# Two layers of block-cached attention and gated MLP on one core: square-block turning on VectorE, a second place for MLP sums, one copy for the last values

## The chip, the cores and the metric

One core of one Trainium2 chip runs the whole program. The metric is the device time of one execution in microseconds, the median of several runs.

## What is computed

A decode step for a batch of 4 rows of 640 numbers, float32, through attention, MLP, attention, MLP, with the same weights in both layers. Each stage norms its input and adds its result to it:

```python
def _A_ref(x, k_cache, v_cache, wq, wo):        # 32 heads of 128, the last W = 1024 cached positions
    q = (x @ wq) -> [B, 32, 1, 128]
    scores = einsum(q, k_cache[:, :, Sk - W:]) * 128 ** -0.5
    o = einsum(softmax(scores), v_cache[:, :, Sk - W:])
    return o.reshape(B, 1, 32 * 128) @ wo
def _B_ref(x, W_gate, W_up, W_down):            # 1728 hidden columns
    gate, up = x @ W_gate, x @ W_up
    return ((gate * (gate > 0)) * up) @ W_down
x = A_x
x = x + _A_ref(_layernorm(x), ...); x = x + _B_ref(_layernorm(x), ...)
x = x + _A_ref(_layernorm(x), ...); x = x + _B_ref(_layernorm(x), ...)
```

## The kernel before

All weights and caches are laid out on the host as rows of 128 partitions: `heads` (queries, keys, values and output weights of the heads in the order of use), `kept` (the five last heads, in two groups K0 and K1) and `mlp`. One list, `plan`, holds 89 pieces of these rows in the order in which SP issues them, each with its place in one large on-chip tile, `store` (128 x 50,624 float32, so one column is 512 B over all partitions). `load()` (L211) issues the next piece as soon as the program order has freed its whole place; the framework's semaphores then hold SP until the last matmul that reads that place is through. A piece counts as landed as a whole.

Layer 0 streams `heads` in pieces of 16,000 columns through three places, then loads all of `kept` and uses it last. The kept heads stay for layer 1, which begins with them (`order`). So the first MLP has little room: seven places of together 7,040 columns, four of them inside the kept rows. Three of these (`AHEAD` 768 columns, `BACK` 1,728, `AWAY` 1,280) hold kept data that ScalarE first copies elsewhere, into `probs`, the PSUM tiles `ps`, `yy`, `po` (columns 128 on), `pp` (the upper halves of its two banks) and the two `banks`, and later back. The first MLP's 25,920 columns go through these places in 28 pieces of 640 to 1,344 columns. The pieces behind them are the first of layer 1's `heads`: five into the places that the MLP leaves (1,280, 1,280, 704, 768, 1,728 columns), the next into places that layer 1's queries free (1,152 and 1,280 columns at the query weights of K0 and K1), and then into those that its scores free (1,024, 2,048, 3,392, 4,096, ...).

Matmuls of all these go through one helper, `product` (L242), which splits a matmul where its columns lie in two pieces.

The work around the change, in program order on each engine:

- `normalized()` (L335 to L357): VectorE sums the rows (L342), TensorE averages, VectorE subtracts (L346, the result `xc` in `gates`), ScalarE squares and sums (L348), TensorE turns `xc` (L352 and L354, into `pp`), and VectorE copies the turned rows to `xT` (L356). The rows lie as four groups of 160 columns at partitions 0, 32, 64 and 96, four batch rows in each.
- `deviation(ss)` (L359): four small matmuls on the sum of squares (L334), a root on ScalarE (L362), a reciprocal on VectorE (L363). In attention it stands before the first `query`; in the MLP behind `gate(3)`.
- `forward()`: `gate(j)` for j = 3, 0, 1, 2 makes a block of gate and up columns in `pp[:, j % 2]`; `gated(j)` applies relu on ScalarE (L552) and the product on VectorE (L553); `hidden(j)` turns the result (TensorE L560, copy on VectorE L561); `down(j)` adds into `y`.
- `fill` (L325) and `busy` (L318) are matmuls without use, into `po`, in the stretches in which `waits[0]` is set.
- `values(..., last)`: the last weighted values are copied from `po` to `gates` by VectorE (L450) and ScalarE (L451), half each; then four transpositions (L470) and `project`.

Of the kernel before, what the change touches and what calls it, by code (L numbers as in the profile page):

```python
# [1 line left out]

# [5 lines left out]
F32 = mybir.dt.float32  # L8
# [54 lines left out]


AHEAD = KEPT * D, KEPT * D + 768
BACK = FRONT - 2 * KV - 1728, FRONT - 2 * KV
AWAY = BACK[0] - 1280, BACK[0]
HOME = 12864
FIRST, MOST = 32640, 16320
LAP = 3 * MOST + 1024  # L70


def size_of(what, i):
    return len(HEADS[i]) * D if what == "q" else D if what == "o" else KV


def spread(parts):
# [11 lines left out]

ROWS = {row: spread(parts) for row, parts in PARTS.items()}  # L90

WHERE = {part: (row, at) for row, (places, _, _) in ROWS.items() for part, at in places.items()}


@with_exitstack
def decode_kernel(ctx: ExitStack, tc: tile.TileContext, x, source, sel, out):
# [28 lines left out]

    def stretch(layer, lo, end, to):

        size = -(-(end - lo) // -(-(end - lo) // MOST) // 64) * 64
        while lo < end:
            hi = min(end, lo + size)  # L130
            if to + hi - lo > LAP:
                to = 0
            to = put(layer, "heads", to, lo, hi)
            lo = hi
        return to
# [23 lines left out]

    f, z, a, q, k = FRONT, STORE - D, AHEAD[0], AWAY[0], BACK[0]  # L160
    assert STORE - FRONT == 2 * 1280 + 64 + D
    gu = [(z, D), (f, 1280), (f + 1280, 1344), (a, 768), (k, 960), (k + 960, 768), (q, 1280)]
    gu_end = [(f, 1280), (f + 1280, 1280), (f + 2560, D)]
    wd = [(a, D), (k, 960), (k + 960, D), (q, 1280), *gu_end, (a, D), (k, D), (k + D, D)]
    lo = 0
# [4 lines left out]


    lo = HELD
    for to, n in (f, 1280), (f + 1280, 1280), (f + 2560, D + 64), (a, 768), (k, 1728):
        put(1, "heads", to, lo, lo + n)
        lo += n
    to = AHEAD[1]
    for n in 1152, 1280, 1024, 2048, 3392:
        to = put(1, "heads", to, lo, lo + n)
        lo += n
    assert to == HOME  # L180
# [94 lines left out]
    nc.scalar.dma_start(out=sel_sb, in_=sel)  # L275


    xT = const.tile([P, KC * B + 28], F32, name="xT")


    qT = const.tile([P, SIDE - 1 + SIDE * SIDE * B], F32, name="qT")
# [4 lines left out]

    ps = ps_s.tile([P, 2, 512], F32, name="ps")
    pp = ps_p.tile([P, 2, 512], F32, name="pp")
    po = ps_o.tile([P, 512], F32, name="po")
    nc.vector.memset(ps, 0.0)  # L290
    nc.vector.memset(po, 0.0)
# [45 lines left out]
    def normalized():  # L337

        ysb, xc, sq = probs[:, :QUARTER], gates[:, :QUARTER], gates[:, QUARTER:2 * QUARTER]
        waits[0] = True  # L340
        su = small.tile([P, 1], F32, name="su", bufs=1)
        nc.vector.tensor_reduce(su, y, axis=AX.X, op=ALU.add)  # L342
        nc.scalar.copy(ysb, y)
        busy(2)
        mu = mean(su)
        nc.vector.tensor_tensor(xc, ysb, mu.to_broadcast([P, QUARTER]), op=ALU.subtract)  # L346
        ss = small.tile([P, 1], F32, name="ss", bufs=1)
        nc.scalar.activation(sq, xc, AF.Square, accum_out=ss)  # L348
        fill(1)

        pt = pp[:, 0, :KC * 32].rearrange("p (c x) -> p c x", c=KC)
        nc.tensor.transpose(pt[:, :4], xc[:, :P], ident)  # L352
        for g in range(4):
            nc.tensor.matmul(pt[32 * g:32 * g + 32, 4, :B], xc[:, P:], ident[:, 32 * g:32 * g + B],  # L354
                             start=True, stop=True, tile_position=(0, 32 * g))
        nc.vector.tensor_copy(xT[:, :KC * B].rearrange("p (c b) -> p c b", b=B), pt[:, :, :B])  # L356
        return ss  # L357

    def deviation(ss):  # L359
# [17 lines left out]
    def query(layer, g, spread=False):  # L377


        n = len(HEADS[g]) * P  # L380
        qp[g] = bank(n)
        for c in range(KC - 1):
            product(qp[g][32 * c:32 * c + 32], xT[:, B * c:B * c + 32], *part(layer, "q", g, c * n, n),
                    start=True, stop=c > 0 and not spread, tile_position=(0, 32 * c))
        part_done(layer, "q", g, 0, (KC - 1) * n)
        c = KC - 1
        m = n // 4 if spread else n
        for a in range(n // m):
            product(qp[g][32 * a:32 * a + 32, a * m:a * m + m], xT[:, B * c:B * c + 32],
                    *part(layer, "q", g, c * n + a * m, m), start=False, stop=True, tile_position=(0, 32 * a))  # L390
        part_done(layer, "q", g, c * n, n)

# [13 lines left out]
    def scores(layer, g):  # L406
        n = len(HEADS[g])
        to = sc[g] = pp if layer and g == order[1][0] else ps
        for i, h in enumerate(HEADS[g]):
            for j in range(2):  # L410
                for b in range(B):
                    lo = (j * B + b) * 512
                    at = SIDE - 1 + SIDE * (B * i + b) - i
                    product(to[32 * b:32 * b + SIDE, j, :], qT[:, at:at + SIDE], *part(layer, "k", h, lo, 512),
                            start=i == 0, stop=i == n - 1, tile_position=(0, 32 * b))
                    part_done(layer, "k", h, lo, 512)
                    if to is pp and k0 + i * KV + lo < HOME + BACK[1] - BACK[0] <= k0 + i * KV + lo + 512:
                        nc.scalar.copy(store[:, HOME:HOME + 1024], ps.rearrange("p j n -> p (j n)"))
                        nc.scalar.copy(store[:, HOME + 1024:HOME + 1408], po[:, P:])
                        nc.scalar.copy(store[:, HOME + 1408:HOME + 1728], yy[:, QUARTER:3 * QUARTER])  # L420
        nm[g] = small.tile([P, 1], F32, name="nm")
        nc.vector.tensor_reduce(nm[g], to.rearrange("p j n -> p (j n)"), axis=AX.X, op=ALU.max, negate=True)  # L422

# [8 lines left out]
    def values(layer, g, last=False):  # L432
# [14 lines left out]
        if last:  # L447
            waits[0] = layer == 0
            fill(1, pp[:, 0])
            nc.vector.tensor_copy(gates[:, 2 * P:], po[:, 2 * P:])  # L450
            nc.scalar.copy(gates[:, :2 * P], po[:, :2 * P])  # L451
            if layer == 0:
                nc.scalar.copy(po[:, P:], store[:, BACK[0] + 1024:BACK[0] + 1408])
                nc.scalar.copy(pp[:, :, 256:], away[:, :512].rearrange("p (j n) -> p j n", j=2))
                free(*BACK)
        else:
            nc.scalar.copy(gates, po)  # L457

    def totals(g):
        so = bank(P)  # L460
# [23 lines left out]
    def attention(layer):  # L484
# [38 lines left out]
        values_turned(gs[-1])  # L523
        if layer == 0:
            for i in range(2):
                nc.scalar.copy(banks[i][:, P:], away[:, 512 + 384 * i:896 + 384 * i])
            free(*AWAY)
            project(layer, gs[-2])
        fill(1)
# [2 lines left out]
    def forward(layer):  # L532
# [3 lines left out]
        def gate(j):  # L536
            n, groups = (P, 4) if j < 3 else (64, 3)
            at = GU0 + j * GU if j < 3 else 0
            gus[j] = pp[:, j % 2, :2 * P]
            for c in range(KC):  # L540
                for g in range(groups):
                    lo = at + (c * groups + g) * 2 * n
                    product(gus[j][32 * g:32 * g + 32], xT[:, B * c:B * c + 32], layer, "mlp", lo, 2 * n,
                            start=c == 0, stop=c == KC - 1, tile_position=(0, 32 * g))
                    done(layer, "mlp", lo, 2 * n)

        def gated(j):
            n, p = (P, P) if j < 3 else (64, 96)
            gu = gus.pop(j)
            at = 256 * (j % 2)  # L550
            a, b = gates[:p, at:at + n], gates[:p, at + P:at + P + n]
            nc.scalar.activation(a, gu[:p, :n], AF.Relu, scale=rstd[:p])  # L552
            nc.vector.scalar_tensor_tensor(b, gu[:p, n:2 * n], rstd[:p], a, op0=ALU.mult, op1=ALU.mult)  # L553
            return b

        def hidden(j, h):
            hTs[j] = small.tile([P, 4, B], F32, name="hT", bufs=4)
            ph = bank(P).rearrange("p (f x) -> p f x", f=4)
            if j < 3:
                nc.tensor.transpose(ph, h, ident)  # L560
                nc.vector.tensor_copy(hTs[j], ph[:, :, :B])  # L561
                return

            for g, lo, f in (0, 0, 0), (1, 64, 0), (2, 0, 1), (2, 64, 1):
                nc.tensor.matmul(ph[lo:lo + 64, f, :B], h, ident[:96, 32 * g:32 * g + B],
                                 start=True, stop=True, tile_position=(0, lo))
            nc.vector.tensor_copy(hTs[j][:, :2], ph[:, :2, :B])

        def down(j, last=False):
            for f in range(4 if j < 3 else 1):  # L570
# [19 lines left out]
        waits[0] = layer == 0  # L590
        rstd = deviation(ss)
        go_on()
        fill(1)
        h = gated(3)
        for j, j1 in (3, 0), (0, 1), (1, 2):
            gate(j1)
            hidden(j, h)
            fill(1)
            h = gated(j1)
        down(3)  # L600
        down(0)
        hidden(2, h)
        if layer == 0:
            nc.scalar.copy(away[:, :512].rearrange("p (j n) -> p j n", j=2), pp[:, :, 256:])
            for i in range(2):
                nc.scalar.copy(away[:, 512 + 384 * i:896 + 384 * i], banks[i][:, P:])
            live[AWAY[0]:AWAY[1]] = [True] * 1280
        down(1)
        down(2, last=True)

# [63 lines left out]
```

## Time and profile before

| | |
|---|---|
| median of 3 runs | 732.33 us (731.74 to 732.71) |
| profiled execution | 734.14 us, of which span 732.4 us |
| busy: TensorE, VectorE, ScalarE | 445.4, 75.2, 54.2 us |
| moved by DMA | 311.19 MB, mean 425 GB/s |
| mean granted TensorE clock | 0.816 |

The span is the time from the first to the last instruction on the core; what lies around it is start and end of the program. All times in the rows are microseconds from the span's start. PEclk is the granted clock as a share of 2.4 GHz: 0.50 is 1.2 GHz, and values between are means over a stretch in which both occur.

### The profile page before, as it was taken

Reading aid. Unit: us, or ns where it says so; the run is one execution under the profiler, and the core shown is the slowest. Engines: PE = TensorE matmul, PEld = TensorE weight load, DVE = VectorE, ACT = ScalarE, POOL = GpSimd, SP = SyncE. Lnnn points to the kernel's source line nnn. Section 1 sums busy time; section 2 is a strip of 40 time slices with the busy share of each in tenths; the row PEclk is TensorE's granted clock in tenths of the full one; section 3 lists DMA queues with packets and bytes.
Section 4 is the critical chain, followed back from the end, with each engine's and each line's share of the span. In section 5 each row is a group of like instructions: output and inputs, shape, how many; then the busy total and the mean of one; then the engine's idle time right before and its main releaser. Section 6 shows DMA issues by size and latency. Waiting matters only on the chain.

```text
span 732.4 us, 8422 instructions
## 1 busy us (share of the span) xinstructions
PE 445.4 (61%) x3844; PEld 158.6 (22%) x3844; DVE 75.2 (10%) x279; ACT 54.2 (7%) x101; POOL 0.2 (0%) x4
## 2 busy tenths in 40 slices
PE   0845565655655554619879896365656555556576
PEld 0211112222112121103344241021121112112123
DVE  1111001010010101002101211001010010101011
ACT  0200000000000000001302210000000000000100
POOL 0000000000000000000000000000000000000000
PEclk9888887776777777759999999677787878778989
DMA  9999999999999999999999999999999999999996
GB/s 405 445 405 438 440 445 416 434 431 444 441 419 428 419 441 448 419 431 425 419 392 407 392 427 455 423 441 434 433 427 444 424 441 426 438 437 420 423 429 286
DMA packets 13291, 311.19 MB, mean 425 GB/s; under 512 B 1476, under 2 KB 1732, under 8 KB 6984
## 3 DMA queue, kind: packets, MB, share of 16 engines
q1 hardware_dynamic: 13104, 310.56, 98.9%
q8 instruction: 30, 0.49, 0.2%
q10 hardware_dynamic: 152, 0.09, 0.0%
q14 instruction: 5, 0.04, 0.0%
HBM read 310.57 MB, written 0.08 MB: 424 GB/s over the span
## 4 chain that ended last, share of the span: by engine, by line
DMA 73%; PE 22%; another core or an unknown queue 3%; DVE 1%; issue 1%; SPq 0%; ACT 0%; DVEq 0%; ACTq 0%
DMA store<-in_heads 57%; DMA store<-in_kept 9%; PE ps L242 9%; DMA store<-in_mlp 7%; PE po L242 6%; PE m L242 2%; PE pp L242 1%; PE y L242 1%; PE pp L430 1%; PE m L401 1%; PE m L470 0%; PE m L461 0%; DVE gates L394 0%; SPq L211 0%
## 5 line engine op out<-in xcount | busy, mean ns | idle before, releaser
L242 PE MATMUL po<-store,pT 128*16 128x512 f32 (+2 forms) x1044 | 155.4, 707 | 130.4 <-DMA store<-in_heads 125.0
L242 PE MATMUL ps<-store,qT 128*4 128x512 f32 (+3 forms) x1016 | 151.7, 682 | 109.9 <-DMA store<-in_heads 89.4
L242 PEld LDWEIGHTS po<-store,pT 128*16 128x16 f32 x1044 | 38.4, 110 | 234.3 <-DMA store<-in_heads 124.7
L242 PEld LDWEIGHTS ps<-store,qT 128*4 128x4 f32 x1016 | 36.3, 94 | 206.7 <-DMA store<-in_heads 99.9
L422 DVE TENSOR_REDUCE nm<-ps 128x1 f32<-128x1024 f32 x17 | 20.8, 1224 | 242.4 <-PE ps L242 242.4
L426 ACT ACTIVATE probs<-ps,nm 128x1024 f32<-128x1024 f32 x17 | 18.9, 1114 | 328.9 <-DVE nm L422 328.9
L242 PE MATMUL m<-store,xT 128*32 128x512 f32 (+5 forms) x152 | 30.3, 600 | 10.5 <-DMA store<-in_heads 10.5
L440 DVE COPY pT<-pp 128x16 f32<-128x16 f32 x128 | 17.1, 168 | 140.2 <-PE po L242 140.2
L457 ACT COPY gates<-po 128x512 f32<-128x512 f32 x16 | 9.4, 586 | 249.5 <-PE po L242 249.5
L242 PE MATMUL pp<-store,xT 128*32 128x256 f32 (+3 forms) x322 | 21.0, 371 | 7.4 <-DMA store<-in_mlp 3.5
L242 PE MATMUL y<-store,oT 128*4 128x160 f32 x512 | 23.3, 314 | 1.3 <-DVE oT L474 1.1
L430 PE MATMUL pp<-sel_sb,probs 128*128 128x128 f32 x144 | 20.4, 289 | 0.0
L430 PEld LDWEIGHTS pp<-sel_sb,probs 128*128 128x128 f32 x144 | 17.9, 150 | 0.0
L463 DVE RECIPROCAL r<-m 128x16 f32<-128x16 f32 x18 | 4.6, 258 | 129.1 <-PE m L461 129.1
L242 PEld LDWEIGHTS y<-store,oT 128*4 128x4 f32 x512 | 13.2, 90 | 9.3 <-issue 3.9
L394 DVE TENSOR_SCALAR gates<-m,rstd 128x512 f32<-128x512 f32 (+2 forms) x18 | 12.4, 690 | 26.6 <-PE m L242 26.6
L242 PEld LDWEIGHTS pp<-store,xT 128*32 128x32 f32 x322 | 11.3, 114 | 15.2 <-DMA store<-in_mlp 6.7
L401 PE MATMUL m<-sel_sb,gates 128*128 128x128 f32 x64 | 12.8, 325 | 0.0
L242 PE MATMUL y<-store,hT 128*4 128x160 f32 (+1 forms) x224 | 11.2, 299 | 2.4 <-DMA store<-in_mlp 2.2
L470 PE MATMUL m<-sel_sb,gates 128*128 128x128 f32 x72 | 12.0, 289 | 0.8 <-DVE gates L450 0.8
L401 PEld LDWEIGHTS m<-sel_sb,gates 128*128 128x128 f32 x64 | 7.9, 159 | 20.0 <-issue 20.0
L242 PEld LDWEIGHTS m<-store,xT 128*32 128x32 f32 x152 | 7.2, 124 | 22.3 <-DMA store<-in_heads 11.7
(80 smaller groups left out, 124.1 us busy)
## 6 DMA issues: line engine op xcount, KB each, us to landing
store<-in_heads SPq DMA_DIRECT2D x22, 8000.0 KB, 45.7
store<-in_heads SPq DMA_DIRECT2D x1, 7776.0 KB, 45.5
store<-in_heads SPq DMA_DIRECT2D x1, 7744.0 KB, 46.0
store<-in_heads SPq DMA_DIRECT2D x1, 7424.0 KB, 44.6
store<-in_heads SPq DMA_DIRECT2D x1, 7360.0 KB, 35.3
store<-in_heads SPq DMA_DIRECT2D x1, 7168.0 KB, 33.6
store<-in_mlp SPq DMA_DIRECT2D x10, 640.0 KB, 7.4
store<-in_heads SPq DMA_DIRECT2D x1, 6400.0 KB, 44.4
```

The costliest lines, as they stand in the source:

```text
L242: nc.tensor.matmul(out[:, a:z], by, t[rows, p:p + z - a], start=start and not a, stop=stop and z == n, **how)
L394: nc.vector.tensor_scalar(gates[:, :len(HEADS[g]) * P], qp.pop(g), rstd, SCALE, op0=ALU.mult, op1=ALU.mult)
L401: nc.tensor.transpose(qt[:, i], gates[:, i * P:(i + 1) * P], ident)
L422: nc.vector.tensor_reduce(nm[g], to.rearrange("p j n -> p (j n)"), axis=AX.X, op=ALU.max, negate=True)
L426: nc.scalar.activation(probs, sc.pop(g).rearrange("p j n -> p (j n)"), AF.Exp, bias=nm.pop(g), accum_out=sums[g])
L430: nc.tensor.transpose(pp[:, c // 4, c % 4 * P:c % 4 * P + P], probs[:, c * P:(c + 1) * P], ident)
L440: nc.vector.tensor_copy(to[:, 4 * j:4 * j + 4], pp[:, j].rearrange("p (c x) -> p c x", c=4)[:, :, i:P:32])
L457: nc.scalar.copy(gates, po)
L463: nc.vector.reciprocal(r[g], so.rearrange("p (b i) -> p i b", b=B)[:, :SIDE])
L470: nc.tensor.transpose(ot[:, 127 * b:127 * b + P], gates[:, b * P:(b + 1) * P], ident)
```

## The change

1. `normalized()`: one VectorE transposition by square blocks of 32 x 32 takes `xc` to `xT`; the TensorE transposition, the four small matmuls and the copy go. `xT` has 160 columns, 32 for each block of the contraction, and the host lays out the rows of `wq`, `W_gate` and `W_up` to match.
2. `hidden(j)` for j < 3: one VectorE transposition by square blocks takes the gated values (now in `probs`) into `gates`, from which `down` reads; the host lays out `W_down` to match. Block 3 is turned as before.
3. The sums of MLP blocks 1 and 3 lie in `po`, those of 0 and 2 in `pp`. Fills in the MLP go to the bank that was not used last. The stash in `po` starts at column 256 instead of 128, that in `pp` is one run of 640 columns (`parked`).
4. So `BACK` has 1,600 columns instead of 1,728, and `AWAY` 1,408 instead of 1,280; the pieces that go there change by 128 columns, and layer 1's piece of 3,392 becomes 3,520.
5. The last values are copied to `gates` by one ScalarE instruction.
6. The pieces of `heads` in the two attention stages are cut at ends of blocks where possible (`fewest`): 15,872 to 16,320 columns instead of 16,000, in the same number.

```diff
-BACK = FRONT - 2 * KV - 1728, FRONT - 2 * KV
-AWAY = BACK[0] - 1280, BACK[0]
-HOME = 12864
+BACK = FRONT - 2 * KV - 1600, FRONT - 2 * KV
+AWAY = BACK[0] - 1408, BACK[0]
+HOME = 12992
...
+def fewest(lo, end, n):
+
+    if n == 1:
+        return (0, [end]) if end - lo <= MOST else (n + len(CUTS), [])
+    most = min(lo + MOST, end)
+    ends = [(most, most not in CUTS)] + [(x, False) for x in CUTS if most - 512 < x < most]
+    return min((fewest(hi, end, n - 1)[0] + cut, [hi, *fewest(hi, end, n - 1)[1]]) for hi, cut in ends)
...
+CUTS = frozenset(ROWS["heads"][2])
+fewest = cache(fewest)
...
-        size = -(-(end - lo) // -(-(end - lo) // MOST) // 64) * 64
-        while lo < end:
-            hi = min(end, lo + size)
+        for hi in fewest(lo, end, -(-(end - lo) // MOST))[1]:
...
-    gu = [(z, D), (f, 1280), (f + 1280, 1344), (a, 768), (k, 960), (k + 960, 768), (q, 1280)]
+    gu = [(z, D), (f, 1280), (f + 1280, 1344), (a, 768), (k, 960), (k + 960, 640), (q, 1408)]
...
-    for to, n in (f, 1280), (f + 1280, 1280), (f + 2560, D + 64), (a, 768), (k, 1728):
+    for to, n in (f, 1280), (f + 1280, 1280), (f + 2560, D + 64), (a, 768), (k, 1600):
...
-    for n in 1152, 1280, 1024, 2048, 3392:
+    for n in 1152, 1280, 1024, 2048, 3520:
...
-    xT = const.tile([P, KC * B + 28], F32, name="xT")
+    xT = const.tile([P, KC * 32], F32, name="xT")
...
+    parked = pp.rearrange("p j n -> p (j n)")[:, 256:896]
...
         fill(1)
-
-        pt = pp[:, 0, :KC * 32].rearrange("p (c x) -> p c x", c=KC)
-        nc.tensor.transpose(pt[:, :4], xc[:, :P], ident)
-        for g in range(4):
-            nc.tensor.matmul(pt[32 * g:32 * g + 32, 4, :B], xc[:, P:], ident[:, 32 * g:32 * g + B],
-                             start=True, stop=True, tile_position=(0, 32 * g))
-        nc.vector.tensor_copy(xT[:, :KC * B].rearrange("p (c b) -> p c b", b=B), pt[:, :, :B])
+        nc.vector.transpose(xT, xc)
         return ss
...
-            nc.vector.tensor_copy(gates[:, 2 * P:], po[:, 2 * P:])
-            nc.scalar.copy(gates[:, :2 * P], po[:, :2 * P])
-            if layer == 0:
-                nc.scalar.copy(po[:, P:], store[:, BACK[0] + 1024:BACK[0] + 1408])
-                nc.scalar.copy(pp[:, :, 256:], away[:, :512].rearrange("p (j n) -> p j n", j=2))
-                free(*BACK)
-        else:
-            nc.scalar.copy(gates, po)
+        nc.scalar.copy(gates, po)
+        if last and layer == 0:
+            nc.scalar.copy(po[:, 256:], store[:, BACK[0] + 1024:BACK[0] + 1280])
+            nc.scalar.copy(parked, away[:, :640])
+            free(*BACK)
...
-            gus[j] = pp[:, j % 2, :2 * P]
+            gus[j] = po[:, :2 * P] if j % 2 else pp[:, 0, :2 * P]
...
-            at = 256 * (j % 2)
-            a, b = gates[:p, at:at + n], gates[:p, at + P:at + P + n]
+            at = P * (j + 1) % 512
+            a, b = gates[:p, at:at + n], probs[:, :P] if j < 3 else gates[:p, 3 * P:3 * P + n]
...
-            hTs[j] = small.tile([P, 4, B], F32, name="hT", bufs=4)
+            if j < 3:
+                hTs[j] = gates[:, P * j:P * j + P].rearrange("p (f x) -> p f x", f=4)[:, :, :B]
+                nc.vector.transpose(gates[:, P * j:P * j + P], h)
+                return
+            hTs[j] = small.tile([P, 2, B], F32, name="hT", bufs=1)
             ph = bank(P).rearrange("p (f x) -> p f x", f=4)
-            if j < 3:
-                nc.tensor.transpose(ph, h, ident)
-                nc.vector.tensor_copy(hTs[j], ph[:, :, :B])
-                return
...
-        fill(1)
+        fill(1, banks[turn_of[0] ^ 1])
         h = gated(3)
         for j, j1 in (3, 0), (0, 1), (1, 2):
             gate(j1)
             hidden(j, h)
-            fill(1)
+            fill(1, banks[turn_of[0] ^ 1])
             h = gated(j1)
```

## Rows read from the trace of the kernel before

**Rows 1.** The page: busy time of each engine, and the chain that ended last, by engine.

```profile
PE 445.4 (61%) x3844; PEld 158.6 (22%) x3844; DVE 75.2 (10%) x279; ACT 54.2 (7%) x101; POOL 0.2 (0%) x4
...
DMA 73%; PE 22%; another core or an unknown queue 3%; DVE 1%; issue 1%; SPq 0%; ACT 0%; DVEq 0%; ACTq 0%
```

**Rows 2.** Windows of four stretches; last columns: granted clock, DMA share, GB/s.

```profile
150.00:350.00 200.00, 111.72 (x905) 38.38 (x903) 19.12 (x74) 10.16 (x17) 0.00 (x0) 0.76 1.00 431
364.00:396.00 32.00, 26.14 (x358) 13.75 (x358) 2.86 (x12) 3.84 (x11) 0.00 (x0) 0.95 1.02 401
396.00:404.00 8.00, 7.53 (x80) 3.43 (x84) 2.21 (x7) 2.47 (x6) 0.00 (x0) 0.79 0.99 389
404.00:408.00 4.00, 4.00 (x40) 0.99 (x36) 0.00 (x0) 1.38 (x3) 0.00 (x0) 1.00 0.88 260
```

**Rows 3.** Windows of 2 us in the first MLP and the queries behind it.

```profile
370.00:372.00 2.00, 1.58 (x34) 0.70 (x24) 0.00 (x0) 0.00 (x0) 0.00 (x0) 1.00 1.01 388
372.00:374.00 2.00, 1.15 (x16) 0.55 (x17) 0.00 (x0) 0.07 (x1) 0.00 (x0) 1.00 0.99 382
374.00:376.00 2.00, 1.89 (x23) 1.25 (x25) 0.42 (x2) 0.30 (x1) 0.00 (x0) 0.69 1.01 364
...
400.00:402.00 2.00, 2.00 (x22) 0.78 (x14) 0.62 (x1) 0.36 (x2) 0.00 (x0) 0.50 1.04 434
```

**Rows 4.** The chain that ended last in order of time: start, length, what.

```profile
1.64 45.70 DMA store<-in_heads
...
341.19 22.73 DMA store<-in_kept
...
389.07 6.98 DMA store<-in_mlp
...
698.16 30.63 DMA store<-in_mlp
```

**Rows 5.** Timeline of layer 1's norm and first query: start, length, engine, line, idle before.

```profile
397.45 0.32 DVE L346 TENSOR_TENSOR gates<-probs,m 128x160 f32<-128x160 f32 x1 [0.52 <-PE m L334]
...
398.05 0.18 ACT L348 ACTIVATION_READ_ACCUMULATOR gates<-gates 128x1 f32 x1
...
398.29 0.24 PE L334 MATMUL m<-ss,sel_sb 128*32 128x1 f32 x8
398.40 0.18 DVE L356 COPY xT<-pp 128x20 f32<-128x20 f32 x1 [0.62 <-PE pp L354]
...
398.63 0.85 PE L242 MATMUL m<-probs,xT 128*32 128x384 f32 x2
...
400.52 0.33 SPq L211 DMA_DIRECT2D store<-in_heads  x1
```

**Rows 6.** Groups by line: busy us, mean ns of one, idle before.

```profile
L422 DVE TENSOR_REDUCE nm<-ps 128x1 f32<-128x1024 f32 x17 | 20.8, 1224 | 242.4 <-PE ps L242 242.4
...
L457 ACT COPY gates<-po 128x512 f32<-128x512 f32 x16 | 9.4, 586 | 249.5 <-PE po L242 249.5
...
L242 PEld LDWEIGHTS ps<-store,qT 128*4 128x4 f32 x1016 | 36.3, 94 | 206.7 <-DMA store<-in_heads 99.9 <-issue 78.7 <-DMA store<-in_kept 20.9
```

**Rows 7.** Timeline of the first MLP's blocks 3, 0 and 1.

```profile
369.27 0.28 DVE L553 SCALAR_TENSOR_TENSOR gates<-pp,rstd,gates 96x64 f32<-96x64 f32 x1 [0.38 <-ACT gates L552]
...
369.61 1.97 PE L242 MATMUL pp<-store,xT 128*32 128x256 f32 x34 [0.65 <-DVE gates L553]
...
374.75 0.20 PEld L242 LDWEIGHTS pp<-store,xT 128*32 128x32 f32 x6 [0.30 <-DVE gates L553]
374.75 3.83 PE L242 MATMUL pp<-store,xT 128*32 128x256 f32 x38
```

**Rows 8.** Timeline of the end of layer 0's attention.

```profile
361.15 0.42 DVE L450 COPY gates<-po 128x256 f32<-128x256 f32 x1 [5.73 <-PE po L242]
361.61 0.37 ACT L451 COPY gates<-po 128x256 f32<-128x256 f32 x1 [3.72 <-DVE gates L450]
...
364.05 0.73 PE L242 MATMUL y<-store,oT 128*4 128x160 f32 x16 [0.20 <-DMA store<-in_kept]
```

More of the change, by code (lines that the diff above doesn't have):

```diff
@@ L1 @@
 from contextlib import ExitStack
+from functools import cache
 import concourse.bass as bass
@@ L382, in query @@
         for c in range(KC - 1):
-            product(qp[g][32 * c:32 * c + 32], xT[:, B * c:B * c + 32], *part(layer, "q", g, c * n, n),
+            product(qp[g][32 * c:32 * c + 32], xT[:, 32 * c:32 * c + 32], *part(layer, "q", g, c * n, n),
                     start=True, stop=c > 0 and not spread, tile_position=(0, 32 * c))
@@ L388, in query @@
         for a in range(n // m):
-            product(qp[g][32 * a:32 * a + 32, a * m:a * m + m], xT[:, B * c:B * c + 32],
+            product(qp[g][32 * a:32 * a + 32, a * m:a * m + m], xT[:, 32 * c:32 * c + 32],
                     *part(layer, "q", g, c * n + a * m, m), start=False, stop=True, tile_position=(0, 32 * a))
@@ L418, in scores @@
                         nc.scalar.copy(store[:, HOME:HOME + 1024], ps.rearrange("p j n -> p (j n)"))
-                        nc.scalar.copy(store[:, HOME + 1024:HOME + 1408], po[:, P:])
-                        nc.scalar.copy(store[:, HOME + 1408:HOME + 1728], yy[:, QUARTER:3 * QUARTER])
+                        nc.scalar.copy(store[:, HOME + 1024:HOME + 1280], po[:, 256:])
+                        nc.scalar.copy(store[:, HOME + 1280:HOME + 1600], yy[:, QUARTER:3 * QUARTER])
         nm[g] = small.tile([P, 1], F32, name="nm")
@@ L525, in attention @@
             for i in range(2):
-                nc.scalar.copy(banks[i][:, P:], away[:, 512 + 384 * i:896 + 384 * i])
+                nc.scalar.copy(banks[i][:, P:], away[:, 640 + 384 * i:1024 + 384 * i])
             free(*AWAY)
@@ L542, in gate @@
                     lo = at + (c * groups + g) * 2 * n
-                    product(gus[j][32 * g:32 * g + 32], xT[:, B * c:B * c + 32], layer, "mlp", lo, 2 * n,
+                    product(gus[j][32 * g:32 * g + 32], xT[:, 32 * c:32 * c + 32], layer, "mlp", lo, 2 * n,
                             start=c == 0, stop=c == KC - 1, tile_position=(0, 32 * g))
@@ L566, in hidden @@
                                  start=True, stop=True, tile_position=(0, lo))
-            nc.vector.tensor_copy(hTs[j][:, :2], ph[:, :2, :B])
+            nc.vector.tensor_copy(hTs[j], ph[:, :2, :B])
         def down(j, last=False):
@@ L603, in forward @@
         if layer == 0:
-            nc.scalar.copy(away[:, :512].rearrange("p (j n) -> p j n", j=2), pp[:, :, 256:])
+            nc.scalar.copy(away[:, :640], parked)
             for i in range(2):
-                nc.scalar.copy(away[:, 512 + 384 * i:896 + 384 * i], banks[i][:, P:])
-            live[AWAY[0]:AWAY[1]] = [True] * 1280
+                nc.scalar.copy(away[:, 640 + 384 * i:1024 + 384 * i], banks[i][:, P:])
+            live[AWAY[0]:AWAY[1]] = [True] * 1408
         down(1)
@@ L624, in arr @@
         return np.asarray(a)
-    rows = [np.arange(g * QUARTER, g * QUARTER + P) for g in range(4)]
-    rows = np.concatenate(rows + [np.arange(g * QUARTER + P, (g + 1) * QUARTER) for g in range(4)])
+    rows = np.arange(D).reshape(4, KC, 32).transpose(1, 0, 2).reshape(D)
     kc, vc = arr(A_k_cache)[:, :, -W:, :], arr(A_v_cache)[:, :, -W:, :]
@@ L645 @@
         wd[n + P:].reshape(64, 2, 2 * QUARTER).transpose(1, 0, 2).reshape(P, 2 * QUARTER),
-        wd[:n].reshape(12, P, D).transpose(1, 0, 2).reshape(P, 3 * WD),
+        wd[:n].reshape(3, 4, 4, 32, D).transpose(1, 3, 0, 2, 4).reshape(P, 3 * WD),
     ], axis=1)
```

## The prediction

> **What bounds the kernel now.** I read the page first, for who is busy and what the last chain is made of. TensorE is busy 61% of the span, VectorE 10%, ScalarE 7%, and 73% of the chain that ended last is transfers [rows 1]. So this kernel goes at the pace of its one stream of transfers, and an edit counts only if it (a) keeps that stream from running dry, (b) changes what the stream costs, or (c) shortens what stands before the first or after the last byte.
>
> Then I cut the span into stretches to see where the stream is below its own pace [rows 2]. In the attention stage it moves 431 GB/s with the DMA engines busy all the time. In the MLP of the first layer it moves 401 over 32 us, in the 8 us behind it 389, and in the next 4 us 260. Against 431 these lose 32 x 30/431 = 2.2 us, 8 x 42/431 = 0.8 us and 4 x 171/431 = 1.6 us: 4.6 us is all that better feeding could return. The share column tells the three apart. In the MLP the DMA engines stay at 1.02: they are busy on pieces of 640 to 1,408 columns (2.5 to 5.6 KB a partition), so most of that loss is the small pieces, not a lack of work. From 404 to 408 the share is 0.88: there the engines lack work.
>
> The chain in order of time fixes the two ends of the MLP stretch: the last kept piece lands at 363.92, the last MLP piece at 389.07 + 6.98 = 396.05, and the last piece of all at 698.16 + 30.63 = 728.79, with only its matmuls, the output copy and its transfer behind it [rows 4].
>
> **Why the stream dries at 404.** Before it, the store is full of kept weights; the next pieces can be issued only into what the MLP left (5,760 columns of 512 B, 2.95 MB or 6.8 us at 431 GB/s), then into what the first queries of layer 1 free. The first such piece is issued at 400.52 [rows 5], when the query matmuls that start at 398.63 are through. So what stands between the last MLP matmul and that query sets the dry stretch, and here the change cuts into the chain.
>
> **The normed rows turned by VectorE.** Removed from each of four `normalized()` calls: one transposition and four small matmuls on TensorE and the copy L356. In layer 1: xc is ready at 397.45 + 0.32 = 397.77; turning and copying take until 398.40 + 0.18 = 398.58; the query starts at 398.63 [rows 5]. Added: one 128x160 VectorE transposition right behind the subtraction on the same engine. No such operation is in this trace. Bounds from rows: not below the 20-element copy's 0.18 us [rows 5], not above the 1,024-element reduction's 1.22 us [rows 6]. The nearest is the 128x160 subtraction itself, 0.32 us [rows 5], and I take that: xT at 398.13.
>
> The Trainium skill ("VectorE: DVE Perf Modes", section "The three transpose paths") gives 311 ns for a 128x128 bf16 VectorE transposition against 390 ns on TensorE, and says it turns only 32x32 blocks; no run so far shows it. By that figure the step would also come to about 0.3 us, an estimate.
>
> That looks like 0.45 us won, but TensorE works in order. `deviation(normalized())` puts the eight L334 matmuls on the sum of squares ahead of the query. They wait for ScalarE, which squares xc and has read out its accumulator at 398.05 + 0.18 = 398.23, and L334 starts at 398.29 for 0.24 us [rows 5]. Nothing of this moves. So the query can start no earlier than about 398.53: **0.1 us** is won of the 0.45; what is late next is the sum of squares. At the upper bound xT would come at 399.03 and the query 0.45 us late.
>
> **Against it: the stash moves 128 columns.** BACK shrinks from 1,728 to 1,600 columns and AWAY grows by as much. BACK's piece is one of those issued before the queries, AWAY's isn't, so the stream holds 128 x 128 x 4 B = 65.5 KB less when it runs dry: **0.15 us** at 431 GB/s lost, the columns coming later in the 3,520-column piece. Every other piece around the MLP keeps its size, and 89 pieces stay 89 in the same order.
>
> **Inside the first MLP.** Here gate(3) follows `normalized()` directly, so it does start earlier, by the whole 0.45 us. Then gate(0) waits today for L553, which ends at 369.27 + 0.28 = 369.55, although both use different halves of `pp` [rows 7]. With odd blocks in `po` that wait goes, and gate(0), which starts at 369.61 after 0.65 us of waiting, could start that and the 0.45 earlier, 1.1 us in all; gate(1) waits for the same instruction of the block before it by 0.3 us [rows 7]. The turned hidden rows lose a transposition and a copy, on TensorE and VectorE, against one VectorE instruction of about 0.3 us. What does it buy? Freed space earlier, so pieces issued earlier, into a queue whose engines are busy already (share 1.02). What is late next is the data: TensorE already waits for MLP pieces. Bounds: nothing, and the 2.2 us of the stretch. The dip behind gate(0)'s late start, 388, 382 and 364 GB/s from 370 to 376 [rows 3], loses 2 x (13 + 19 + 37)/401 = 0.35 us against the stretch's 401; as its share is 0.99 to 1.01, I take **0.2 us**.
>
> **At no cost or gain, and what hides it.** The copy of the last values becomes one ScalarE instruction: VectorE then ScalarE, 361.15 to 361.98, becomes one of 0.59 us [rows 6, 8], 0.25 us sooner for the instructions queued behind on ScalarE (the stash copies and their two frees), while the first two transpositions wait 0.2 us longer. The projection behind it waits until 364.05 for the kept piece that lands at 363.92 [rows 4, 8]; without that cover it is worth 0.2 us. In layer 1 the stream covers it. The pieces of the two attention stages are cut at block ends (15,872 to 16,320 columns instead of 16,000): the same number and bytes, and some thirty fewer split matmuls on an engine that waits for data; uncovered, their sixty extra weight loads (an f32 matmul shows as two) at 0.1 us each [rows 6] would be worth 6 us. The MLP of layer 1 ends on its data [rows 4]; earlier hidden rows don't move the last piece, and matmuls, copy and output after it are as before. The start is hidden by the first 45.70 us transfer [rows 4].
>
> **Sum.** -0.1 + 0.15 - 0.2 = -0.15 us. The profiled execution took 734.14 us (span 732.4, 1.74 around it) and would become 734.0; the median of the runs, 732.33, lies 1.8 below, so 732.2. A measurement of this kernel tells about 0.2% (1.5 us) from no change.
>
> **Rivals.**
> *The dry stretch closes.* Were the queries through 1.5 us or more earlier, the 1.6 us at 404 to 408 and the 0.35 us in the MLP would come back: 732.3 - 1.6 - 0.35 = 730.4. For it: TensorE ran much of the queries at half clock, a granted 0.50 from 400 to 402 [rows 3]; the 1.9 us from the query's start at 398.63 to the first free at 400.52 and the second query behind it could take about half at 1.00. Against it: nothing in the change makes the stretch before busier. 17%, with the cases of partial gain over 0.2%.
> *TensorE cools.* The edit takes 26 matmuls and transpositions (five in each of four norms, six for hidden rows) out of stretches where fills are put in to keep TensorE at 2.4 GHz. If the granted clock is 0.50 in two more gate blocks and through the whole of the norm and query, each block takes 1.7 us longer (34 matmuls in 1.97 us at gate(0), 38 in 3.83 at gate(1), mostly at 0.50 [rows 7]: 0.04 us more each, over forty), and the pieces it frees come late by that; it decides once frees are over 1.5 us late, and gives 732.3 + 1.7 = 734.0. The Trainium skill ("TensorE: Matmul & The Clock Gate", section "What's actually happening") says "the default state is throttled, and activity releases the throttle"; the trace agrees as far as the fall to 0.50 follows stretches with gaps. Against it: with gate(1) at half clock the share still was 1.01 from 374 to 376 [rows 3]. 4%.
> *The turn is dear.* A VectorE transposition delays the query by what it takes over 0.8 us; from 2.3 us on it deepens the dry stretch by more than 1.5 us, 733.9. The dearest VectorE row is 1.22 us. 3%.
> *Hidden, as summed.* 76%, its own range 731.0 to 733.2.
>
> So faster by over 0.2% 17%, within 76%, slower 7%. The range reaches to the first rival's time and, above, takes in the upper bound of the transposition (0.45 us at the query, 0.15 of the stash) and as much again for the spread of single runs: 730.4 to 733.4.
>
> **What would show it.** Right: L334 ahead of the query starts within 0.1 us of where it did after the subtraction; the rate from 404 to 408 (as counted from the last MLP matmul) stays under 330 GB/s; gate(0) no longer waits for L553 but for data; the last piece lands within 1 us of 728.8. Wrong: a share under 0.95 inside the MLP before, which I read as none; a query that starts 0.4 us sooner; another pace than 431 GB/s in the attention stages, where I expect the new cuts to change nothing.

## The result and the profile after

The changed kernel takes 735.52 us, the median of six runs (735.38 to 736.97); the kernel before, timed beside it, takes 732.11 (six runs, 731.71 to 732.71). The ratio is 1.005 [1.0037, 1.0063]: 3.4 us slower, where 732.2 and a range of 730.4 to 733.4 were predicted. The profiled execution took 735.54 us, close to its median.

The page of the kernel after, against [rows 1]: its span, the busy time of each engine, the shares of two DMA queues (packets, MB, share of 16 engines' span) and the chain by engine.

```profile
span 733.8 us, 8267 instructions
PE 442.0 (60%) x3764; PEld 144.5 (20%) x3764; DVE 76.1 (10%) x277; ACT 54.6 (7%) x101; POOL 0.2 (0%) x4
...
q1 hardware_dynamic: 13104, 310.56, 99.0%
q8 instruction: 29, 0.48, 0.3%
...
DMA 77%; PE 20%; another core or an unknown queue 1%; issue 1%; DVE 0%; SPq 0%; ACT 0%; DVEq 0%
```

TensorE's records have 80 matmuls fewer and 3.4 us less busy time, and the kernel is still longer. 77% of the last chain is transfers, and q1 carries the same number of packets and bytes as in the kernel before, whose line is:

```profile
q1 hardware_dynamic: 13104, 310.56, 98.9%
```

So the place to look is the stream.

Windows of the kernel after; the stretches are those of [rows 2].

```profile
150.00:350.00 200.00, 110.91 (x894) 34.64 (x892) 19.14 (x74) 10.16 (x17) 0.00 (x0) 0.79 1.00 429
364.00:396.00 32.00, 25.18 (x351) 12.67 (x354) 3.89 (x14) 5.12 (x14) 0.00 (x0) 1.00 1.02 396
396.00:404.00 8.00, 7.00 (x98) 3.10 (x101) 2.37 (x7) 2.47 (x6) 0.00 (x0) 1.00 0.99 377
404.00:408.00 4.00, 4.00 (x42) 0.99 (x38) 0.00 (x0) 1.47 (x3) 0.00 (x0) 1.00 1.00 402
```

Two things are to be seen. The attention stage, where the change only moves the cuts between pieces, goes at 429 GB/s at a share of 1.00, not 431 [rows 2]: the DMA engines are as busy and move half a per cent less. Over the whole 730 us, 2 parts in 431 would be 3.4 us. And the dry stretch is gone: 402 GB/s at 404 to 408 for 260, and the granted clock is 1.00 from 396 to 404 for 0.79. Yet the kernel is slower.

The chain of the kernel after in order of time (start, length), for comparison with [rows 4]; the kept piece in it is an earlier one than the kept piece there:

```profile
340.01 20.29 DMA store<-in_kept
...
390.61 7.28 DMA store<-in_mlp
...
699.16 31.03 DMA store<-in_mlp
```

The last piece lands at 699.16 + 31.03 = 730.19, 1.4 us later than in the profiled execution of before [rows 4]. That execution had taken 734.14 us, 2.0 more than the median beside which the change is timed; those are the other 2 us of the 3.4.

The timeline of layer 1's norm and first query, for [rows 5]:

```profile
399.30 0.32 DVE L357 TENSOR_TENSOR gates<-probs,m 128x160 f32<-128x160 f32 x1 [0.52 <-PE m L345]
399.65 0.34 DVE L361 STREAM_TRANSPOSE xT<-gates 128x160 f32<-128x160 f32 x1
...
400.13 0.24 PE L345 MATMUL m<-ss,sel_sb 128*32 128x1 f32 x8 [0.55 <-ACT gates L359]
400.22 0.49 PE L252 MATMUL m<-probs,xT 128*32 128x384 f32 x2
```

The subtraction ends at 399.62, the query starts at 400.22: 0.60 us, against 398.63 - 397.77 = 0.86 before [rows 5]. The eight L345 matmuls on the sum of squares still stand ahead of the query and wait for ScalarE; `xT` is ready at 399.65 + 0.34 = 399.99, before them. The query starts 0.09 us after the first of the eight, without waiting for the end of their 0.24 us.

The timeline of the first MLP, for [rows 7]:

```profile
370.04 1.16 PE L252 MATMUL pp<-store,xT 128*32 128x256 f32 x20
...
371.76 0.64 PE L252 MATMUL pp<-store,xT 128*32 128x192 f32 x8 [0.56 <-DMA store<-in_mlp]
...
374.30 1.06 PE L252 MATMUL pp<-store,xT 128*32 128x128 f32 x12 [1.10 <-DMA store<-in_mlp]
```

`gate(0)` starts at 370.04 without a wait for VectorE, and what stops it now is data: the two waits shown, 0.56 and 1.10 us, and one of 0.17 us between them.

### The profile page after: what moved, and what is told of

Same layout as the page of the kernel before. It is cut to its first block, busy times and chain, and to the rows that moved or that the text cites. A ratio compares the mean times of both kernels' runs of the same rounds, so it can differ in the third digit from the quotient of the medians.

```text
span 733.8 us, 8267 instructions
## 1 busy us (share of the span) xinstructions
PE 442.0 (60%) x3764; PEld 144.5 (20%) x3764; DVE 76.1 (10%) x277; ACT 54.6 (7%) x101; POOL 0.2 (0%) x4
## 4 chain that ended last, share of the span: by engine, by line
DMA 77%; PE 20%; another core or an unknown queue 1%; issue 1%; DVE 0%; SPq 0%; ACT 0%; DVEq 0%
DMA store<-in_heads 60%; PE ps L252 9%; DMA store<-in_mlp 9%; DMA store<-in_kept 9%; PE po L252 5%; PE m L252 2%; PE y L252 1%; PE pp L252 1%; PE pp L435 1%; PE m L406 1%; PE m L472 0%; PE m L463 0%; PE y L378 0%; DVE gates L399 0%
## 5 line engine op out<-in xcount | busy, mean ns | idle before, releaser
L252 PE MATMUL po<-store,pT 128*16 128x512 f32 (+1 forms) x1026 | 156.9, 715 | 125.0 <-DMA store<-in_heads 118.7
L252 PEld LDWEIGHTS po<-store,pT 128*16 128x16 f32 x1026 | 34.2, 110 | 233.7 <-issue 111.5
L252 PEld LDWEIGHTS ps<-store,qT 128*4 128x4 f32 x996 | 29.7, 93 | 211.5 <-DMA store<-in_heads 98.0
L252 PE MATMUL m<-store,xT 128*32 128x512 f32 (+4 forms) x150 | 28.6, 576 | 11.0 <-DMA store<-in_heads 11.0
L252 PE MATMUL pp<-store,xT 128*32 128x256 f32 (+3 forms) x172 | 13.7, 412 | 6.0 <-DMA store<-in_mlp 6.0
L399 DVE TENSOR_SCALAR gates<-m,rstd 128x512 f32<-128x512 f32 (+2 forms) x18 | 12.4, 690 | 25.4 <-PE m L252 25.4
L252 PE MATMUL y<-store,gates 128*4 128x160 f32 x192 | 9.6, 299 | 2.7 <-DMA store<-in_mlp 2.5
```

Source lines behind the costliest of these rows:

```text
L252: nc.tensor.matmul(out[:, a:z], by, t[rows, p:p + z - a], start=start and not a, stop=stop and z == n, **how)
L399: nc.vector.tensor_scalar(gates[:, :len(HEADS[g]) * P], qp.pop(g), rstd, SCALE, op0=ALU.mult, op1=ALU.mult)
```

## The experiments

Nothing in these views names a part of the change that costs 3.4 us. What the prediction did not look at is where the tiles lie. In the kernel before, `store` begins in the built program at byte 9,472 of each partition, 37 x 256; the eight columns (32 bytes) of `pad`, a tile that nothing uses, lie in front of it. The change makes `xT` 448 bytes larger and the tiles `hT` together 224 smaller, so `store`, into which all 89 pieces go, begins at byte 9,696, 224 past a multiple of 256 and 32 past a multiple of 64. Every piece begins at a multiple of 64 columns (256 bytes) inside `store`, so where `store` begins decides for all of them; `first_q`, right behind it, moves along. The theory, A in the expectations, is that the place of `store` costs the 3.4 us, and the edits themselves nothing. Against it stand the new cuts, which touch most of the stream, and the rest of the change. All kernels compute the whole reference.

**e1: before, with `store` 32 bytes further** (byte 9,504).

```diff
-    big.tile([P, 8], F32, name="pad")
+    big.tile([P, 16], F32, name="pad")
```

> The kernel before with one edit: the unused tile in front of the store has 16 columns instead of 8, so the store begins at byte 9,504 of each partition (32 past a multiple of 64) instead of 9,472 (a multiple of 256). Theory A (the changed kernel is slower because its larger turned-rows tile moves the store to byte 9,696, again 32 past a multiple of 64, and each packet of the stream then takes longer): the packets of the profile after take about 3.8 ns more each (5,120 B: 200 ns against 196), 720 data packets a DMA engine, so +2.7 us, about 734.8 us; 431 GB/s in the attention stage becomes 429. Rival B (the changed work itself costs the time: cuts, sums in another tile, turning): no change, 732.1 us within 0.5.

735.42 us (735.25 to 735.69) beside 731.93: 1.0042 [1.0031, 1.0054]. An unused tile 32 bytes larger costs all that the change costs.

**e2: after, without `pad`** (byte 9,664: a multiple of 64, 192 past one of 256).

```diff
-    big.tile([P, 8], F32, name="pad")
```

> The changed kernel without the unused tile in front of the store, so the store begins at byte 9,664, a multiple of 64 but not of 256. Theory A with 64 as the step that matters: 735.5 - 2.7 = 732.8 us or less. Theory A with 256: as the changed kernel, 735.5. Rival B: 735.5.

735.02 us (734.74 to 736.89), 1.0044 [1.0032, 1.0056]. A multiple of 64 does not bring the time back.

**e3: before, `pad` of 24 columns** (byte 9,536, 64 past a multiple of 256).

> The kernel before with 24 columns in the unused tile: the store begins at byte 9,536, a multiple of 64 but 64 past a multiple of 256. Theory A with 64 as the step: 732.1 us, no change. Theory A with 256: about 734.8. Rival B: 732.1.

734.82 us (734.69 to 734.85), 1.0034 [1.0022, 1.0046]. The same from the other side: the step lies above 64 bytes.

**e4: before, with the new cuts alone** (`fewest`, `CUTS` and the loop in `stretch` from the diff; byte 9,472).

> The kernel before with the new cuts of the attention stages' pieces alone (15,872 to 16,320 columns at ends of blocks), the store at byte 9,472. Theory A and the prediction: hidden, 732.1 us within 0.5. A rival of its own, that the new sizes or places of the pieces cost the stream its pace: up to 735.5.

732.1 us (731.54 to 734.0, 12 runs), 1.0003 [0.9994, 1.0011]. The cuts cost and bring nothing. Its windows:

```profile
396.00:404.00 8.00, 7.62 (x100) 3.34 (x96) 2.21 (x7) 2.47 (x6) 0.00 (x0) 1.00 1.01 395
404.00:408.00 4.00, 4.00 (x35) 0.96 (x28) 1.22 (x1) 2.08 (x4) 0.00 (x0) 1.00 1.03 422
```

With the norm, the queries and the MLP of before, this execution has no dry stretch either: 422 GB/s, clock 1.00.

**e5: after, with `store` on a multiple of 256** (byte 9,728; 64 columns are taken from `first_q`, so that all fits).

```diff
-HELD = 4288
+HELD = 4224
...
-    big.tile([P, 8], F32, name="pad")
+    big.tile([P, 16], F32, name="pad")
```

> The changed kernel with the store put back on a multiple of 256: byte 9,728 of each partition. The room for it comes from the tile of the first query weights, which holds 64 columns fewer (4,224), so layer 1 streams 64 columns more (33 KB, 0.08 us at 431 GB/s). Theory A (placement, now with 256 as the step, since a store on a multiple of 64 alone cost 2.9 us): 732.0 us, 3.4 below the changed kernel; GB/s in the attention stage back at 431. Rival B (some of the changed work costs time as well): between 732.5 and 735.5.

732.08 us (731.75 to 734.22, 11 runs), 1.0006 [0.9997, 1.0015]. This is the whole change without its cost. Its windows and two pieces of its chain:

```profile
150.00:350.00 200.00, 111.90 (x895) 34.78 (x893) 19.13 (x74) 10.17 (x17) 0.00 (x0) 0.77 1.00 431
364.00:396.00 32.00, 25.70 (x355) 12.47 (x355) 3.50 (x12) 3.88 (x11) 0.00 (x0) 1.00 1.02 405
...
404.00:408.00 4.00, 3.91 (x32) 0.96 (x24) 1.27 (x2) 2.38 (x4) 0.00 (x0) 1.00 1.05 431
```

```profile
339.58 19.22 DMA store<-in_kept
...
695.70 30.64 DMA store<-in_mlp
```

Attention goes at 431 GB/s again, at the same share of 1.00. The kept piece lands 1.5 us before the same piece in the kernel after (358.80 for 360.30), the last piece of all 3.85 us before it (726.34 for 730.19): the loss grows along the stream. It does not grow with the bytes alone: from 364 to 396, where the pieces are small and the packets many, it is 2.2% (396 GB/s for 405), in attention 0.5%.

**e6: before, `pad` of 40 columns** (byte 9,600, 128 past a multiple of 256).

> The kernel before with the store at byte 9,600, 128 past a multiple of 256. Theory A with 256 as the step: about 734.9 us, as at 64 past it. Theory A with 128 as the step: 731.9 us.

734.72 us (734.43 to 736.53), 1.0043 [1.003, 1.0055]. 128 does not do either; both places on multiples of 256 do, 9,472 and 9,728, and they are 256 bytes apart.

The trace keeps a record of each packet, of its bytes and of how long it took. A piece is 128 packets, one to a partition; with `first_q` that makes 90 x 128 = 11,520, 720 on each of the 16 DMA engines. Median durations in ns, and the durations of all packets together, as the mean of an engine, in us:

```
               bytes past  packet of ... bytes         instruction  packets per  all packets,
               n x 256     5,120 12,288 49,152 57,344  read 16 KB   DMA engine   us per engine
e4 (before)         0        196    460   1815   2116      938          720         725.4
e5 (after)          0        196    460   1815   2116      938          720         725.2
e1 (before)        32        200    464   1819   2120     1073          720         728.6
e3 (before)        64        199    462   1818   2119     1073          720         728.2
e6 (before)       128        196    465   1819   2121     1072          720         727.9
e2 (after)        192        198    462   1818   2119     1069          720         729.0
after             224        200    464   1819   2120     1073          720         728.7
e7 (before)         0        196    460      -      -      934         1432         734.4
e8 (before)        32        200    464      -      -     1078         1432         739.7
```

The medians rise by 2 to 5 ns, whether a packet holds 5 or 57 KB; only that of the 5,120-byte packets at 128 past stays. On the multiple 97% of the data packets take just the median of their size or less. Off it, of the packets whose size also occurs there, those that take longer than that median are 79% in after (224 past), 74% in e1 (32), 69% in e3 (64), 68% in e2 (192) and 51% in e6 (128). The surplus is not quite the same for all sizes: in after it averages 3.0 ns under 6 KB and 5.1 ns above 40 KB, leaving out the 1% of packets, as many on the multiple, that take over 20 ns more. So more than ten times the bytes cost less than twice as much.

The sums hold the whole loss: 728.7 - 725.2 = 3.5 us for after against e5, where the times differ by 3.44; 728.6 - 725.4 = 3.2 for e1 against e4, where they differ by 3.3. In after against e5 the 720 data packets of an engine make 3.2 us of it, 4.4 ns each in the mean, and the instruction reads, which do not go into `store`, 29 x 135/16 = 0.24 us. (The row of e2 is not of the same kind as the others: its profiled execution has a dry stretch, see e9.) The page shows the instruction reads too: q8 takes 0.3% of the span in the kernel after, and in e5 less:

```profile
q8 instruction: 29, 0.48, 0.2%
```

If the cost is one for each packet, it should about double with their number.

**e7 and e8: twice the packets**, at byte 9,472 and, with `pad` of 16 columns as well, at 9,504. Each piece goes as two transfers of half its columns.

```diff
-            nc.sync.dma_start(out=store[:, to:to + hi - lo], in_=source[row][:, lo:hi])
+            mid = (hi - lo) // 128 * 64
+            nc.sync.dma_start(out=store[:, to:to + mid], in_=source[row][:, lo:lo + mid])
+            nc.sync.dma_start(out=store[:, to + mid:to + hi - lo], in_=source[row][:, lo + mid:hi])
```

> The kernel before with each piece of the plan issued as two transfers of half the columns, store on a multiple of 256: twice the packets. In the trace before, a packet takes about 8 ns beyond its bytes, so 720 more a DMA engine cost 5.8 us: about 737.7 us, if SP keeps up. The base for the next run.

> As the run with halved pieces, with the store 32 bytes past a multiple of 64. Theory A1 (the misplaced store costs a fixed time for each packet): with twice the packets the loss doubles, 7 us over the halved run on its multiple of 256. Theory A2 (it costs by the byte, or by the transfer's end alone): 3.5 us over it.

e7: 738.62 us (737.85 to 739.77), 1.0093 [1.0079, 1.0107]. e8: 745.1 us (742.89 to 746.59), 1.0171 [1.0152, 1.0191]. The same 32 bytes cost 6.5 us at 1,432 packets an engine and 3.5 at 720: 1.9 times for 2.0 times the packets at the same bytes. With four runs each, and intervals that reach 1.0 and 1.4 us to either side, the 6.5 is uncertain by about 1.7 us, which still leaves out the 3.5 of a cost by the byte. The packet durations of the trace hold 5.4 us of it; for the data packets alone it is 5.1 us against 2.9 between e1 and e4, 1.7 times. So the cost goes mostly by packets, A1, and not by the byte. The other half of A2, a cost at each transfer's end, these two runs cannot tell from A1, since halving doubles the transfers as well; that single packets take longer speaks against it. The packets of both pages are the same and their rates differ, e7 first, then e8:

```profile
DMA packets 26109, 311.21 MB, mean 422 GB/s; under 512 B 2900, under 2 KB 7892, under 8 KB 15192
```

```profile
DMA packets 26109, 311.21 MB, mean 418 GB/s; under 512 B 2900, under 2 KB 7892, under 8 KB 15192
```

**e9: before, without any `fill` or `busy` matmul** (only matmuls whose result nobody reads are left out, in both helpers). It asks where the dry stretch of the profiled execution came from, and why its loss in the trace of after paid nothing. Theory D is that it belongs to executions in which TensorE runs layer 1's norm and queries at half clock, and that the usual execution has neither.

```diff
-            for _ in range(n):
+            for _ in range(0):
```

> The kernel before without any of its fills, the matmuls without use that keep TensorE busy around the norms and in the first MLP; the store stays on its multiple of 256. Theory D (the dry stretch at 404 to 408 in the profile of the kernel before belongs to executions in which TensorE runs layer 1's first queries at a granted 0.50; the usual execution has neither): without fills the clock is 0.50 at the queries every time, the stretch is dry every time, and the median rises by what the profiled execution lies above the median, 2.1 us, to about 734 us. Rival (the dry stretch is there in every execution, whatever the clock): 732 us, no change.

734.5 us (733.64 to 735.42) beside 732.37: 1.003 [1.0017, 1.0042]. Its windows:

```profile
396.00:404.00 8.00, 6.76 (x70) 3.24 (x68) 2.21 (x7) 2.47 (x6) 0.00 (x0) 0.57 0.98 368
404.00:408.00 4.00, 4.00 (x40) 0.87 (x36) 0.00 (x0) 0.94 (x2) 0.00 (x0) 1.00 0.91 291
```

Without the fills TensorE idles more (busy 20.2 us from 364 to 396, 25.4 in e4), the granted clock from 396 to 404 is 0.57 (mostly 1.2 GHz) where e4 has 1.00, the stream falls to 291 GB/s at a share of 0.91, and the time rises by 2.1 us: what the profiled execution of before showed [rows 2] and what it lay above its median. The chains say where the 2.1 us are. In e9:

```profile
388.38 7.27 DMA store<-in_mlp
...
398.47 3.52 PE m L242 x26
...
697.77 31.07 DMA store<-in_mlp
```

In e4:

```profile
388.70 7.00 DMA store<-in_mlp
...
398.29 1.86 PE m L252 x26
...
695.87 30.66 DMA store<-in_mlp
```

The first MLP's last piece lands at the same time (395.65 and 395.70), the 26 matmuls of layer 1's first query take 3.52 us for 1.86, and the last piece of all lands 2.3 us later (728.84 for 726.53). In the profiled execution of before the query takes 3.52 us as well:

```profile
398.63 3.52 PE m L242 x26
```

One more trace has this. The profiled execution of e2 took 736.57 us, 1.55 above its median; its query and its dry stretch:

```profile
399.87 3.14 PE m L251 x26
```

```profile
404.00:408.00 4.00, 4.00 (x40) 1.03 (x44) 0.30 (x1) 0.34 (x1) 0.00 (x0) 1.00 0.92 302
```

So of the nine kernels with whole pieces the three whose query takes over 3 us move 260 to 302 GB/s from 404 to 408, and the six at 1.68 to 1.86 us move 388 to 431. And e2 has the norm of the kernel after: the change does not keep the stretch away.

## Why the prediction was wrong

**The step that failed** stands under "Against it" and "At no cost or gain": "Every other piece around the MLP keeps its size, and 89 pieces stay 89 in the same order", "the same number and bytes", and hence no change of the 431 GB/s. The number and the bytes did stay, and the stream still became dearer. Way (b) by which an edit counts, "changes what the stream costs", got no term for where in the partition the pieces land, though the diff resizes two tiles that lie ahead of `store` and the kernel carries an unused tile of 32 bytes right in front of it. That term is 3.4 us, and the packet durations hold all of it: 3.2 us from 720 data packets an engine, 0.24 from the instruction reads. The edits by themselves are worth nothing that can be measured: 735.42 for before (e1) and 735.52 for after off the multiple, 1.0006 [0.9997, 1.0015] on it (e5).

**None of the rivals was the cause.** *The turn is dear*: no, 0.34 us. *TensorE cools*: no, 1.00 from 364 to 404. *The dry stretch closes*: it is absent in the trace of after, and the kernel is slower. e4 has the old norm and no dry stretch, e2 the new norm and a dry stretch, so its absence is not the change's doing; and by e9 the median of before, which the time is measured against, did not pay for it.

**The sum's base.** The prediction summed against an execution 1.8 us above the median of its runs, noted the distance and did not ask what it was. By e9 it was the half clock and the dry stretch, and the prediction spent its first rival, 17%, on getting back what the executions near the median do not lose. That rival asks for queries through "1.5 us or more earlier"; the clock alone does that, 3.52 us at half and 1.86 at full. The prediction's sign "stays under 330 GB/s" failed for the same reason, at 402, or 423 when the window is moved with the last MLP matmul to 405.8.

**What held.** The transposition: 0.32 us taken, 0.34 measured (0.31 for the 128x128 of the hidden rows). What is late next is the sum of squares: its first matmul starts 0.51 us after the subtraction for 0.52. The query itself won 0.26 us where the prediction has 0.1, because it does not wait for the end of the eight matmuls; it is not the clock, since e4, at 1.00, has 0.85 from the subtraction to the query. (The prediction's 398.13 and 399.03 for `xT` are 0.04 us more than the terms beside them; nothing hangs on that.) `gate(0)` starts 2.70 us after its norm's subtraction (367.34 to 370.04) for 3.86 before (365.75 to 369.61), the 1.1 us forecast, and meets data.

**The signs.** Two of the prediction's own signs pointed at the failed step: "another pace than 431 GB/s in the attention stages" was named as the mark of a mistake, and came; the last piece landed 1.4 us late where 1 was allowed. That cuts, turns, banks and the single copy come to nothing together, to within 0.2 us below and 1.1 above, is what e5 shows; the small terms of the sum (0.1, 0.15, 0.2 us) are below what the runs can tell one by one.

**Left open.** Why instruction reads slow down with the place of `store`. Why at 128 past only half of the packets pay and at 32 or 224 past three quarters or more; the medians of the times go the same way (734.7 at 128; 734.8 and 735.0 at 64 and 192; 735.4 and 735.5 at 32 and 224), but that these 0.8 us are the place and not the spread of runs is not shown. And 1.1 us of the 6.5 between e7 and e8, which the packet durations do not hold; about 0.5 us of it is engines with less to do (a share of 0.87 from 404 to 408 in e8; none under 0.96 in e7's 4-us windows from 396 to 420).

## What to carry to other kernels

When a kernel goes at the pace of its transfers, work out where the large target tile begins before and after any edit that resizes a tile ahead of it. Keep it, and the pieces in it, on a multiple of 256 bytes; an odd-looking unused tile may be there for that. A rate that falls at a full DMA share, with the same packets to move, points to dearer packets and not to a lack of work: look at packet durations. And before summing against a profiled execution, find out what sets it off from the median.

## What the runs showed of the hardware

For transfers from HBM into an on-chip tile, the place of the target matters by steps of 256 bytes: 32, 64, 128, 192 and 224 past a multiple measured 734.7 to 735.5 us, 0 past it 732.1 (two kernels, e4 and e5). The medians of the records are 4 ns higher at 32 past and at 224 past alike. The Trainium skill ("DMA: Bandwidth & Descriptors", section "How a descriptor splits into AXI transactions") says that a descriptor that does not start on a multiple of 256 bytes begins with a transaction from the multiple below; in its example of 576 bytes that makes four transactions instead of three. The section speaks of reading. The traces here agree on the step, for a place that is written; they do not bear out, for such a place, the section's count of beats, by which 224 past would waste seven beats of 32 bytes and 32 past one.

Splitting the same bytes into twice the packets cost 6.7 us in e7, with the target on the multiple: 9 ns in the mean for each of 712 more packets an engine, about twice what misplacing adds to one. It is not spread evenly: from 364 to 396, with the smallest pieces, e7 goes at 361 GB/s where e4 has 406, from 420 to 700 at 432 where e4 has 433.
